# Twelve weight blocks converted inside attention in place of ten, two under way at a time, each loaded three units ahead

## The chip, the cores and the metric

One core of one Trainium2 chip. The time is device microseconds (us) of one execution. PE is the matrix engine (TensorE), "PEld" its weight loads, DVE is VectorE, ACT is ScalarE, POOL is GpSimd; SP issues nearly all DMAs. The outputs are float32. The weights of the two dense parts are stored as 64-bit floats.

## The reference, cut to what matters

```python
# attention: 4 batches, 8 heads, 576 queries and keys, head size 64
scores = scale * (q @ k.T)
scores = where(scores >= max(scores) - tau, scores, -1e9)
attn = exp(scores - max(scores)); attn = attn / (sum(attn) + 1e-9)
x = (attn @ v)            # gathered to 2304 tokens x 512
# first dense part, d_ff = 2048 (w_in, w_out)
h = x @ w_in
y = (h * tanh(softplus(h))) @ w_out
# second dense part, d_ff = 1536 (w_a, w_b, w_out)
out = ((y @ w_a) * (y @ w_b)) @ w_out
```

## The kernel before, in words

**Attention** is written as one loop over 80 units; its order on every engine is kept as written. A unit is 128 queries of two heads. The two heads of one batch make a round of five units, c0 to c4 (c4 holds the last 64 queries of both heads and is half as large), so there are 16 rounds. In step n of the loop:

- DVE copies the scores of unit n out of PSUM with a running minimum (`least`, L266, one per head), and applies the threshold to unit n-1 (`mask`, L285, one per head). In c2 it also scales an older pair's result (`send`, L362, tile `u`), and in the last four rounds, again in c2, it splits a piece of the next phase's input (`first_x`, L72 `xlfirst`).
- ACT takes the exponentials (L278) and copies transposed tiles out of PSUM (L322).
- PE transposes unit n-2 (L321, `tp`), multiplies unit n-4 with v (L340, L344, tile `sums_o`), and computes the scores of unit n+1 (L258, in c4 L260, tile `sp`). There are two `sp` buffers, one per head, so scores of unit n+1 wait until `least` has emptied those of unit n.

**Weights.** Each of the 68 weight blocks (128 x 512) is loaded as 64-bit words (L90, tile `raww`, two buffers) and turned by seven operations into a high and a low fp32r part: ACT L95 (`uw`), DVE L97 and L102 (`aw`), POOL L106 (adds `uw` into `aw`), ACT L108 (`fw`), DVE L110, ACT L112 (high part), DVE L114 (low part). The tiles `uw`, `aw`, `fw` have one buffer each. Blocks of w_in and w_out are called f_0 and f_1, for f = 0 to 15.

`convert` in the attention loop does the first blocks: it starts a block (only the load) at unit T0 = 1 and every PACE units after, and in each later step takes the number of operations that GROUPS lists. The rest are ordinary program after attention (`load_w1` in the first steps of the first dense part, then `after`). Outside attention the framework's scheduler orders the instructions by its own estimate of the time, and it also lets work of the dense part into the last units of attention.

**First dense part.** Tokens go in six tiles of 384. For each of 8 weight blocks f of a half, 12 matmuls make `hm` (L135 to L137, named hm_tile_f), ACT and DVE make `ghm` and `glm` (L178 to L180), and three steps later 12 matmuls add into four `acc` tiles, named with the tile and f of their input. The `acc` tiles take over PSUM that `sums_o` held. At the end of a tile ACT copies them out (L542). Before the last pair's `send` DVE waits for a DMA (`inv`).

Of the kernel before, what the change touches and what calls it, by code (L numbers as in the profile page):

```python
# [22 lines left out]
DFF1, DFF2 = 2048, 1536  # L23
FC1, FC2 = DFF1 // 128, DFF2 // 128
WA, WB = 16, 20
T0, PACE, EARLY = 1, 8, 5
NM = 384
TILES = NT // NM
SCALE = 1.0 / 8.0
# [5 lines left out]
def tile_attn_mish_bilinear(ctx, tc, qd, kd, vd, vd2, tau, w_in, w_out, w_a, w_b, w_out2, out):  # L35
    nc = tc.nc
    V, A, G, PE = nc.vector, nc.scalar, nc.gpsimd, nc.tensor
# [36 lines left out]
    def weight(pool, bufs, src, name, lo_eng):  # L74

        shape = [128, CC, 128]
        out = pool.tile([128, 2, CC, 128], F32R, tag="w", name=name, bufs=bufs)
        tl = lambda s, dt: cv.tile(shape, dt, tag="cv" + s, name=s + name, bufs=1)
        if src.dtype == F32:
            f = tl("f", F32)
            nc.sync.dma_start(out=f, in_=src)
        else:
            raw = cv.tile([128, CC, 256], U32, tag="wraw", name="raw" + name, bufs=2)
            nc.sync.dma_start(out=raw, in_=src.bitcast(U32))  # L90
            words = raw.rearrange("p c (n t) -> p t c n", t=2)
            hi, lo = words[:, 1], words[:, 0]
            u, a, f = tl("u", I32), tl("a", I32), tl("f", F32)
            yield A
            A.activation(u, lo, AF.Copy, scale=2.0 ** -29)  # L95
            yield V
            V.tensor_scalar(  # L97
                out=a, in0=hi.bitcast(I32), scalar1=3, scalar2=0x3FFFFFF8,
                op0=ALU.logical_shift_left, op1=ALU.bitwise_and,
            )  # L100
            yield V
            V.scalar_tensor_tensor(  # L102
                out=a, in0=hi.bitcast(I32), scalar=-0x40000000, in1=a, op0=ALU.bitwise_and, op1=ALU.bitwise_or
            )
            yield G
            G.tensor_tensor(out=a, in0=a, in1=u, op=ALU.add)  # L106
            yield A
            A.activation(f, hi.bitcast(F32), AF.Square)  # L108
            yield V
            V.scalar_tensor_tensor(out=f, in0=f, scalar=TINY, in1=a.bitcast(F32), op0=ALU.is_ge, op1=ALU.mult)  # L110
        yield A
        A.activation(out[:, 0], f, AF.Copy)  # L112
        yield lo_eng
        lo_eng.tensor_tensor(out=out[:, 1], in0=f, in1=f32(out[:, 0]), op=ALU.subtract)  # L114
        return [(out[:, 0, c], out[:, 1, c]) for c in range(CC)]
# [7 lines left out]
    def w1_stages(f, i, pool, bufs, eng):  # L123
        w, block = ((w_in, column_block), (w_out, row_block))[i]
        w1[f][i] = yield from weight(pool, bufs, block(w, f), f"w1{f}_{i}", eng)
# [58 lines left out]
    with late_pools:  # L184
# [188 lines left out]
                split(*x0[c], xs["raw"], V)  # L373

        conv = [w1_stages(f, i, wa_p, WA, V) for f in range(EARLY) for i in range(2)]
        GROUPS = (0, 1, 1, 1, 2, 1, 1, 1)
        active = []

        def convert(start):

            for item in list(active):
                stages, k = item
                for _ in range(GROUPS[k]):
                    if next(stages, None) is None:
# [83 lines left out]
    def w2_steps():  # L468
        slots = iter([(wb_p, WB)] * 4 + [(wa_p, WA)] * 16 + [(wb_p, WB)] * 16)
        for f in range(FC2):  # L470
            for i, (w, block) in enumerate(((w_a, column_block), (w_b, column_block), (w_out2, row_block))):
                stages = weight(*next(slots), block(w, f), f"w2_{f}_{i}", V)
                while True:
                    try:
                        next(stages)
                    except StopIteration as end:
                        w2[f][i] = end.value
                        break
                yield
# [157 lines left out]
```

## Time and profile before

| | |
|---|---|
| time, median of 3 runs | 1163.65 us (1163.05 to 1164.02) |
| the profiled execution's own time | 1163.93 us |
| its span, first to last instruction | 1162.0 us |
| granted PE clock, mean | 0.996 |
| busy over the span: PE, PEld, DVE, ACT, POOL | 98%, 89%, 53%, 47%, 13% |
| attention, to the last scores of PE; first matmul of the dense part | 282.43 us; 286.76 us |

A busy PE is not PE at its peak: ends of matmuls are modelled, so spacing from start to start says more than busy time. The clock column gives the granted PE clock of a stretch as a part of 2.4 GHz (0.50 is 1.2 GHz). DVE and ACT are busy in the first 415 us and mostly idle after it.

### The profile page before, as it was taken

What the parts mean: (1) busy time and instruction counts of PE and PEld (TensorE: products, weight loads), DVE (VectorE), ACT (ScalarE), POOL (GpSimd) and SP (SyncE); (2) the same over time, 40 slices, a digit from 0 to 9 for tenths busy, and PEclk for the clock granted to TensorE, in tenths of its full rate; (3) what the DMA queues carried; (4) which work ended last, traced back from release to release, by engine and by line L of the source; (5) the groups of instructions that cost most, each with busy time, mean ns of one, the idle gap of its engine ahead of it and who ended that gap; (6) DMA issues with size and microseconds to landing.
All of it is one profiled execution on the core that took longest, in us unless ns stands there. A gap on an engine that the chain in (4) does not pass through costs nothing.

```text
span 1162.0 us, 18631 instructions
## 1 busy us (share of the span) xinstructions
PE 1140.0 (98%) x7154; PEld 1038.2 (89%) x7154; DVE 616.9 (53%) x1236; ACT 548.5 (47%) x1111; POOL 148.0 (13%) x154
## 2 busy tenths in 40 slices
PE   9999999999899999999999999999999999999998
PEld 7666666666799999999999999999999999999998
DVE  6899898888699951797222187412121121121111
ACT  6888888877676753575222255312121121221211
POOL 1222222211133320232000023100000000000000
PEclk9999999999999999999999999999999999999999
DMA  4535545534455531465112154101010010100000
GB/s 146 147 108 160 150 123 154 165 115 146 125 169 157 166 124 42 131 203 160 61 49 68 56 177 149 46 1 55 1 56 1 1 56 1 46 9 1 28 1 28
DMA packets 65943, 104.03 MB, mean 90 GB/s; under 512 B 5696, under 2 KB 49984, under 8 KB 65856
## 3 DMA queue, kind: packets, MB, share of 16 engines
q1 hardware_dynamic: 65568, 102.56, 28.6%
q8 instruction: 56, 0.92, 0.3%
q10 hardware_dynamic: 288, 0.30, 0.1%
q14 instruction: 31, 0.25, 0.1%
HBM read 83.89 MB, written 18.95 MB: 88 GB/s over the span
## 4 chain that ended last, share of the span: by engine, by line
PE 74%; DVE 10%; ACT 6%; DMA 5%; issue 4%; POOL 1%; SPq 0%; DVEq 0%; ACTq 0%; POOLq 0%
PE acc L135 8%; PE acc L136 8%; PE acc L137 7%; PE sums_o L340 5%; PE sp L258 5%; PE tp L321 5%; PE hb L135 4%; PE ha L137 4%; PE ha L135 4%; PE hb L137 4%; PE ha L136 4%; PE hb L136 4%; PE hm L135 3%; PE hm L137 3%; PE hm L136 3%
## 5 line engine op out<-in xcount | busy, mean ns | idle before, releaser
L569 DVE TENSOR_TENSOR s<-hb,s 128x384 f32<-128x384 f32 x72 | 40.1, 557 | 275.5 <-PE hb L137 275.5
L106 POOL TENSOR_TENSOR aw<-aw,uw 128x512 int32<-128x512 int32 x68 | 105.9, 1557 | 364.1 <-DVE aw L102 321.6
L180 DVE TENSOR_TENSOR glm<-hsm,ghm 128x384 fp32r<-128x384 f32 x96 | 81.5, 849 | 107.9 <-ACT ghm L179 107.7
L135 PE MATMUL acc<-ghm,w 128*128 128x384 f32 x384 | 130.4, 340 | 5.3 <-ACT y L542 3.1
L136 PE MATMUL acc<-glm,w 128*128 128x384 f32 x384 | 129.4, 337 | 0.0
L137 PE MATMUL acc<-ghm,w 128*128 128x384 f32 x384 | 129.3, 337 | 0.0
L568 ACT ACTIVATE s<-ha 128x384 f32<-128x384 f32 x72 | 35.3, 490 | 186.9 <-PE ha L137 186.9
L266 DVE TENSOR_SCALAR_CACHE_REDUCE s<-sp 128x576 f32<-128x576 f32 x144 | 103.8, 754 | 28.4 <-PE sp L258 24.3
L137 PE MATMUL hm<-xhm,w 128*128 128x384 f32 x352 | 118.0, 335 | 0.0
L135 PE MATMUL hm<-xhm,w 128*128 128x384 f32 x352 | 118.0, 335 | 0.0
L136 PE MATMUL hm<-xlm,w 128*128 128x384 f32 x352 | 118.0, 335 | 0.0
L278 ACT ACTIVATE ex<-s,m 128x576 f32<-128x576 f32 x144 | 109.3, 771 | 9.9 <-DVE s L266 9.5
L322 ACT ACTIVATE pt<-tp 128x512 f32<-128x512 f32 (+1 forms) x192 | 91.3, 488 | 26.4 <-PE tp L321 24.7
L285 DVE SCALAR_TENSOR_TENSOR pm<-s,te,ex 128x576 f32<-128x576 f32 x128 | 99.4, 814 | 0.0
L135 PE MATMUL acc<-gh,w 128*128 128x384 f32 x288 | 96.3, 336 | 2.3 <-DVE y L540 1.6
L71 ACT ACTIVATE gh<-s 128x384 fp32r<-128x384 f32 x72 | 37.7, 523 | 127.5 <-DVE s L569 127.5
L178 ACT ACTIVATE hsm<-hm 128x384 f32<-128x384 f32 x96 | 46.6, 486 | 107.5 <-PE hm L137 107.5
L136 PE MATMUL acc<-gl,w 128*128 128x384 f32 x288 | 96.7, 336 | 0.5 <-DVE gl L72 0.5
L135 PE MATMUL ha<-xhy,w 128*128 128x384 f32 x288 | 96.6, 335 | 0.0
L137 PE MATMUL ha<-xhy,w 128*128 128x384 f32 x288 | 96.6, 335 | 0.0
L136 PE MATMUL ha<-xly,w 128*128 128x384 f32 x288 | 96.6, 335 | 0.0
L137 PE MATMUL hb<-xhy,w 128*128 128x384 f32 x288 | 96.6, 335 | 0.0
(86 smaller groups left out, 2421.6 us busy)
## 6 DMA issues: line engine op xcount, KB each, us to landing
raww<-w_out SPq DMA_DIRECT2D x28, 512.0 KB
v<-vd SPq DMA_DIRECT2D x16, 576.0 KB
raww<-w_in SPq DMA_DIRECT2D x16, 512.0 KB
raww<-w_a SPq DMA_DIRECT2D x12, 512.0 KB
raww<-w_b SPq DMA_DIRECT2D x12, 512.0 KB
xrm<-xd SPq DMA_DIRECT2D x28, 192.0 KB
v<-vd SPq DMA_DIRECT2D x16, 320.0 KB
qr<-qd SPq DMA_DIRECT2D x15, 320.0 KB
```

What stands on the lines that cost most here:

```text
L106: G.tensor_tensor(out=a, in0=a, in1=u, op=ALU.add)
L135: PE.matmul(ps, wh, xh, start=start, stop=False)
L136: PE.matmul(ps, wh, xl, start=False, stop=False)
L137: PE.matmul(ps, wl, xh, start=False, stop=stop)
L180: V.tensor_tensor(out=g[1], in0=hs, in1=f32(g[0]), op=ALU.subtract)
L258: PE.matmul(sp[:, half, 0:288], d["qs"][r, cols], d["k"][r, keys], start=True, stop=True)
L266: V.tensor_scalar(out=u["s"][:, h].rearrange("p (a c) -> p a c", a=2), in0=u["sp"][h][:, :, 0:288], scalar1=1.0, scalar2=None, op0=ALU.mul ...
L278: A.activation(u["e"][:, h], u["s"][:, h], AF.Exp, bias=u["m"][:, h:h + 1], scale=-1.0)
L285: V.scalar_tensor_tensor(out=u["pm"].rearrange("p a c -> p (a c)")[:, h * S:(h + 1) * S], in0=u["s"][:, h], scalar=u["te"][:, h:h + 1], in ...
L321: PE.transpose(tp[:, i], pm[:, j0 + i], ident)
L322: return lambda: A.activation(pt[:, j0:j0 + m], tp[:, :m], AF.Copy)
L340: PE.matmul(po[r], v[0][:, j + 4 * h, r], pair[pi][c & ~1][:, :, j + 4 * h], start=j == 0, stop=j == 4)
```

## The change

```diff
-T0, PACE, EARLY = 1, 8, 5
+T0, PACE, EARLY = 1, 6, 6
...
             nc.sync.dma_start(out=raw, in_=src.bitcast(U32))
             words = raw.rearrange("p c (n t) -> p t c n", t=2)
             hi, lo = words[:, 1], words[:, 0]
+            yield A
             u, a, f = tl("u", I32), tl("a", I32), tl("f", F32)
-            yield A
             A.activation(u, lo, AF.Copy, scale=2.0 ** -29)
...
-        GROUPS = (0, 1, 1, 1, 2, 1, 1, 1)
+        GROUPS = (0, 0, 1, 2, 2, 1, 1, 1)
```

A block now starts every 6 units in place of 8, and the blocks 0_0 to 5_1 (EARLY = 6) are done in the loop, in place of 0_0 to 4_1. Counted from its start unit, a block's L95 comes 3 units later (before: 2), L97 with L102 at 4 (before: 3 and 4), L106 with L108 at 5, L110 at 6, L112 at 7, L114 at 8, as before. The single tiles `uw`, `aw`, `fw` are taken at L95 and no longer at the load, so that the next block's load can be out before the last one is done. The block started at unit 67 is the last and ends at unit 75; before, the one started at 73 ended at 81.

How the instructions move, at three places. The first is DVE around c2 of the fifteenth round, from `least` of unit 72 to that of unit 74. Before (w_0_3102 is block 4_0):

```order
L266 TENSOR_SCALAR s_2_3379,m_2_3355<-sp_2_0_3359 128x576
L266 TENSOR_SCALAR s_2_3379,m_2_3355<-sp_2_1_3360 128x576
L285 SCALAR_TENSOR_TENSOR pm_1_3317,sm_3273<-s_1_3337,te_1_3316,ex_1_3347 128x576 x2
L362 TENSOR_TENSOR u_3037<-u_3037,inv_3194 128x576
L72 TENSOR_TENSOR xlfirst_169<-xr_3334,xhfirst_168 128x384
L266 TENSOR_SCALAR s_3_3424,m_3_3401<-sp_3_0_3404 128x576
L266 TENSOR_SCALAR s_3_3424,m_3_3401<-sp_3_1_3405 128x576
L114 TENSOR_TENSOR w_0_3102<-fw_0_3107,w_0_3102 128x512
L285 SCALAR_TENSOR_TENSOR pm_2_3358,sm_3273<-s_2_3379,te_2_3356,ex_2_3394 128x576 x2
```

With the change (aw_1_3365 is block 5_1, aw_0_3855 block 6_0, which is already the scheduler's):

```order
L266 TENSOR_SCALAR s_2_3418,m_2_3393<-sp_2_0_3397 128x576
L266 TENSOR_SCALAR s_2_3418,m_2_3393<-sp_2_1_3398 128x576
L285 SCALAR_TENSOR_TENSOR pm_1_3353,sm_3309<-s_1_3375,te_1_3352,ex_1_3385 128x576 x2
L362 TENSOR_TENSOR u_3070<-u_3070,inv_3230 128x576
L72 TENSOR_TENSOR xlfirst_169<-xr_3372,xhfirst_168 128x384
L266 TENSOR_SCALAR s_3_3464,m_3_3440<-sp_3_0_3443 128x576
L266 TENSOR_SCALAR s_3_3464,m_3_3440<-sp_3_1_3444 128x576
L110 SCALAR_TENSOR_TENSOR fw_1_3366<-fw_1_3366,aw_1_3365 128x512
L285 SCALAR_TENSOR_TENSOR pm_2_3396,sm_3309<-s_2_3418,te_2_3394,ex_2_3433 128x576 x2
L97 TENSOR_SCALAR aw_0_3855<-raww_0_3852 128x512
```

In unit 73 L110 of a block stands where L114 stood; its POOL addition (L106) is therefore in unit 72, beside `u`. A first operation of block 6_0 follows in the same unit.

The second place is DVE in units 76 and 77, c1 and c2 of the last round. Before (block 4_1 alone):

```order
L266 TENSOR_SCALAR s_1_3559,m_1_3538<-sp_1_0_3541 128x576
L266 TENSOR_SCALAR s_1_3559,m_1_3538<-sp_1_1_3542 128x576
L97 TENSOR_SCALAR aw_1_3467<-raww_1_3464 128x512
L285 SCALAR_TENSOR_TENSOR pm_0_3504,sm_3502<-s_0_3516,te_0_3501,ex_0_3531 128x576 x2
L266 TENSOR_SCALAR s_2_3601,m_2_3577<-sp_2_0_3581 128x576
L266 TENSOR_SCALAR s_2_3601,m_2_3577<-sp_2_1_3582 128x576
L102 SCALAR_TENSOR_TENSOR aw_1_3467<-raww_1_3464,aw_1_3467 128x512
L285 SCALAR_TENSOR_TENSOR pm_1_3540,sm_3502<-s_1_3559,te_1_3539,ex_1_3569 128x576 x2
L362 TENSOR_TENSOR u_3264<-u_3264,inv_3417 128x576
L72 TENSOR_TENSOR xlfirst_171<-xr_3556,xhfirst_170 128x384
```

With the change (w_0_3851 is block 6_0, aw_1_3869 block 6_1):

```order
L266 TENSOR_SCALAR s_1_3594,m_1_3573<-sp_1_0_3576 128x576
L110 SCALAR_TENSOR_TENSOR fw_0_3856<-fw_0_3856,aw_0_3855 128x512
L266 TENSOR_SCALAR s_1_3594,m_1_3573<-sp_1_1_3577 128x576
L285 SCALAR_TENSOR_TENSOR pm_0_3538,sm_3536<-s_0_3551,te_0_3535,ex_0_3566 128x576 x2
L97 TENSOR_SCALAR aw_1_3869<-raww_1_3866 128x512
L114 TENSOR_TENSOR w_0_3851<-fw_0_3856,w_0_3851 128x512
L102 SCALAR_TENSOR_TENSOR aw_1_3869<-raww_1_3866,aw_1_3869 128x512
L266 TENSOR_SCALAR s_2_3635,m_2_3612<-sp_2_0_3616 128x576
L266 TENSOR_SCALAR s_2_3635,m_2_3612<-sp_2_1_3617 128x576
L285 SCALAR_TENSOR_TENSOR pm_1_3575,sm_3536<-s_1_3594,te_1_3574,ex_1_3604 128x576 x2
L362 TENSOR_TENSOR u_3300<-u_3300,inv_3457 128x576
L110 SCALAR_TENSOR_TENSOR fw_1_3870<-fw_1_3870,aw_1_3869 128x512
```

Four operations of the scheduler's blocks 6_0 and 6_1 stand in unit 76 where one stood, and one in unit 77 as before. Up to the `least` of unit 79 DVE now has all four operations of fourteen blocks and one of a fifteenth, in place of nine blocks and two operations of the tenth.

The third place is PE at the end of hm_0_5, the sixth product of the first tile. Before:

```order
L135 MATMUL hm_0_5_4041<-xhfirst_170,w_0_3823 128x384
L136 MATMUL hm_0_5_4041<-xlfirst_171,w_0_3823 128x384
L137 MATMUL hm_0_5_4041<-xhfirst_170,w_0_3823 128x384
L135 MATMUL acc_0_3964<-ghm_0_0_3818,w_1_614 128x384
L136 MATMUL acc_0_3964<-glm_0_0_3819,w_1_614 128x384
L137 MATMUL acc_0_3964<-ghm_0_0_3818,w_1_614 128x384
```

With the change:

```order
L137 MATMUL hm_0_5_4041<-xhfirst_170,w_0_2949 128x384
L135 MATMUL hm_0_6_4072<-xhfirst_164,w_0_3851 128x384
...
L137 MATMUL hm_0_6_4072<-xhfirst_170,w_0_3851 128x384
L135 MATMUL hm_0_7_4131<-xhfirst_164,w_0_3898 128x384
L136 MATMUL hm_0_7_4131<-xlfirst_165,w_0_3898 128x384
L137 MATMUL hm_0_7_4131<-xhfirst_164,w_0_3898 128x384
L135 MATMUL hm_0_7_4131<-xhfirst_166,w_0_3898 128x384
L135 MATMUL acc_0_3964<-ghm_0_0_3846,w_1_525 128x384
```

All 12 matmuls of hm_0_6 and 4 of hm_0_7 come ahead of the first `acc`; before, hm_0_6 came 36 matmuls of `acc` later.

## Rows read from the trace of the kernel before

**Rows 1.** Busy time by stretch; columns: PE, PEld, DVE, ACT, POOL (instructions), clock, DMA

```profile
0.00:282.43 282.43, 274.54 (x2170) 181.75 (x2170) 247.23 (x653) 229.26 (x464) 57.00 (x93) 0.99 0.47 141
...
412.00:1162.00 750.00, 741.74 (x4265) 739.49 (x4265) 257.26 (x420) 230.47 (x472) 48.20 (x33) 1.00 0.18 59
```

**Rows 2.** Timeline of PE, scores of units c0 alone; columns: start, length

```profile
21.79 1.24 PE L258 MATMUL sp<-k,qs 64*128 64x288 f32 x8
...
38.63 1.24 PE L258 MATMUL sp<-k,qs 64*128 64x288 f32 x8
...
73.13 1.24 PE L258 MATMUL sp<-k,qs 64*128 64x288 f32 x8
...
91.62 1.24 PE L258 MATMUL sp<-k,qs 64*128 64x288 f32 x8
...
108.46 1.24 PE L258 MATMUL sp<-k,qs 64*128 64x288 f32 x8
...
126.16 1.24 PE L258 MATMUL sp<-k,qs 64*128 64x288 f32 x8
...
177.25 1.24 PE L258 MATMUL sp<-k,qs 64*128 64x288 f32 x8
...
194.66 1.24 PE L258 MATMUL sp<-k,qs 64*128 64x288 f32 x8
...
211.74 1.24 PE L258 MATMUL sp<-k,qs 64*128 64x288 f32 x8
...
232.08 1.24 PE L258 MATMUL sp<-k,qs 64*128 64x288 f32 x8
...
250.34 1.24 PE L258 MATMUL sp<-k,qs 64*128 64x288 f32 x8
...
269.05 1.24 PE L258 MATMUL sp<-k,qs 64*128 64x288 f32 x8
```

**Rows 3.** Groups of DVE instructions until 282.43 us: busy us, mean ns

```profile
L266 DVE TENSOR_SCALAR_CACHE_REDUCE s<-sp 128x576 f32<-128x576 f32 x143 | 103.0, 754 | 28.3 <-PE sp L258 24.3
L285 DVE SCALAR_TENSOR_TENSOR pm<-s,te,ex 128x576 f32<-128x576 f32 x124 | 96.3, 814 | 0.0
...
L102 DVE SCALAR_TENSOR_TENSOR aw<-raww,aw 128x512 int32<-128x512 int32 x10 | 6.9, 688 | 0.0
```

**Rows 4.** Line L362: duration ns, minimum, median, maximum

```profile
L362 DVE TENSOR_TENSOR u<-u,inv x16: 751/754/1826, 49.7 to 314.8; 128x576 f32<-128x576 f32 x16
```

**Rows 5.** Timeline of DVE and POOL, unit 22 (c2 of the fifth round)

```profile
84.21 1.83 DVE L362 TENSOR_TENSOR u<-u,inv 128x576 f32<-128x576 f32 x1
...
83.55 1.87 POOL L106 TENSOR_TENSOR aw<-aw,uw 128x512 int32<-128x512 int32 x1
```

**Rows 6.** Timeline of PE in attention; in brackets: idle before, and releaser

```profile
88.88 1.37 PE L321 MATMUL tp<-ident,pm 128*128 128x128 f32 x8 [0.76 <-ACT u L349]
...
225.85 1.24 PE L260 MATMUL sp<-k,qs 128*128 128x288 f32 x4 [0.80 <-DVE s L266]
...
227.96 1.82 PE L321 MATMUL tp<-ident,pm 128*128 128x128 f32 x8 [0.77 <-ACT u L349]
```

**Rows 7.** Stretches of 25 us around the two falls of the clock

```profile
225.00:250.00 25.00, 22.47 (x163) 14.40 (x163) 20.91 (x56) 19.42 (x40) 3.69 (x7) 0.93 0.59 174
300.00:325.00 25.00, 21.78 (x129) 20.43 (x126) 16.29 (x27) 12.78 (x28) 6.45 (x5) 0.93 0.48 148
```

**Rows 8.** Timeline of PE at the start of the first dense part

```profile
295.55 0.65 PE L321 MATMUL tp<-ident,ph 128*128 128x128 f32 x4 [0.80 <-ACT pt L322]
...
309.50 0.44 PE L135 MATMUL acc<-ghm,w 128*128 128x384 f32 x1 [2.26 <-ACT u L349]
...
323.94 0.44 PE L135 MATMUL hm<-xhfirst,w 128*128 128x384 f32 x1 [0.96 <-ACT w L112]
```

**Rows 9.** Waits from 320 to 430 us: total us, times, longest

```profile
PE acc L135 <- ACT y L542: 2.0, 3, 0.7
```

**Rows 10.** Timeline of DVE, the last pair's send

```profile
314.81 0.76 DVE L362 TENSOR_TENSOR u<-u,inv 128x576 f32<-128x576 f32 x1 [5.24 <-DMA inv<-rd]
```

## The prediction

> **What bounds the kernel now.** I read the stretches first. After 412 us PE does 4265 matmuls in 750 us, one in 0.176 us, with next to no gap [rows 1]; nothing of the change reaches there. Attention is less plain: until 282 us PE counts as busy for 274.5 us, DVE for 247.2 and ACT for 229.3 of 282.4 [rows 1]. So I took the rhythm of PE, the starts of the scores of c0. Two of the rounds shown take 16.84 us (from 21.79 and from 91.62) and none less [rows 2]; a floor that comes back to the hundredth I take for PE's own work. From 21.79 to 269.05 us lie 14 rounds, 247.26 us, where 14 floors make 235.76: attention loses 11.5 us, and it loses them in single rounds. Which conversion work fell into a round tells what each kind costs, and that is my price list.
>
> **Price list** (round time less 16.84) [rows 2].
> - POOL's addition L106 falls in c2, beside `u`: units 20 to 24 take 18.49, a loss of **1.65**. There `u` took 1.83 us, where 0.75 is usual, and ended with the addition (83.55 to 85.42) [rows 4, 5]. This happened twice in 16 (`u` at most 1826 ns); the other case, with a split in the same unit, is units 60 to 64: 20.34, a loss of **3.50**, of which about 1.75 is PE at half clock (25 us at a mean of 0.93) [rows 7].
> - A split in c2 without that: 1.42 (65 to 69) and 1.87 (70 to 74, with L114 in c3).
> - L114 in c3: 17.70, 0.86 (30 to 34). L97 in c2 and L102 in c3: 17.41, 0.57 (50 to 54). One such operation in c2: 17.08, 0.24 (55 to 59).
>
> The reason is visible in the loads of DVE. In c2 it has two copies of 0.75, two masks of 0.81 and `u`, 0.75 [rows 3, 4]; neighbours overlap by some 0.08, so 3.5 us, when a unit lasts 3.37 on average. What is added there is late in c3 and holds back the next scores and transposes.
>
> **The change, part by part.**
>
> *Loads three units ahead.* They can only save waits of ACT for `raww`; their worth is within the rounds below. SP issues as many DMAs as before, in another order.
>
> *Positions.* Block j starts at 1+6j, so its L106 is in unit 6+6j (before 6+8j). In c2 that is j = 1, 6, 11: units 12, 42, 72. Before it was j = 2, 7: units 22, 62. Three collisions in place of two, and the third again meets a split (units 62, 67, 72, 77 have one). L97 and L102 now follow each other, 1.2 us at 0.69 each as an upper bound [rows 3]; they meet c2 or c3 in four rounds.
>
> *Rounds from unit 5 to 74, new.* Two collisions, 1.65 each, and 0.3 each because L97 precedes L102 just ahead of them: 3.9. Collision with split, 3.5 and 0.3: 3.8. Four rounds with L97 and L102 in c2 or c3 (15, 20, 45, 50), 0.57 each: 2.3. L114 in c2 (25, 55) and L110 in c2 (35), 0.24 each: 0.7. L114 in c3 (30): 0.86. Units 60 to 64, split with L114 in c3: 1.87. Units 65 to 69, split with L110: 1.42. Units 5 to 9: none. Sum 14.85, against 11.50: **+3.3 us**.
>
> *The last round.* Blocks 6_0 and 6_1 now come here. In unit 76 DVE has two copies, two masks and four conversion operations: 1.35 + 1.48 + 4 x 0.55 = 5.0 us. In unit 77 it has 3.5, one operation of 0.6 and the split, 0.5: 4.6. With 3.4 us a unit, DVE is 2.8 late at unit 78. Of the 1.07 + 0.61 late in units 20 to 24, PE paid 1.65, so lateness at c3 is paid nearly whole; with 0.4 for what DVE has in hand in unit 75, 2.4. Bounds: nothing, since the last round held two such operations and a split before too, and its last scores came 13.4 us after 269.05, four units at 3.35; and 2.8. I take **+2.4**, as units 20 to 24 are the nearest rows.
>
> *The start of the dense part.* PE waits 2.26 us for the first `acc`, until ACT's L349 has emptied `sums_o`, and then runs at half clock: 25 us at 0.93 are 1.75 lost [rows 7, 8]. With the change 16 matmuls, 16 x 0.176 = 2.8 us, stand ahead of that `acc`, and block 6_0 that they need is done in unit 76. The wait is covered if L349 is no later. On ACT it now follows the last small copy by eight instructions in place of ten. Gain 2.26 + 1.75 = **4.0** (bounds 0 and 4.0). The wait of 0.96 for hm_0_7's weights [rows 8] goes, as 7_0 is now among the blocks begun in attention: **1.0** (bounds 0 and 1.0). The wait of 0.80 at 295.55 for a copy of ACT [rows 8] should go, since fewer conversions stand before that copy: **0.8** (bounds 0 and 0.8).
>
> *Later.* DVE and ACT have four to five blocks less between 315 and 412 us. The three waits of 0.7 for ACT's L542 are at ends of tiles [rows 9]; the last of them falls after conversion has ended: **0.7**.
>
> **Sum** against the profiled 1163.93: + 3.3 + 2.4 - 4.0 - 1.0 - 0.8 - 0.7 = -0.8, so 1163.1; the median lies 0.28 below the profiled execution. I forecast **1163.0 us, no change**.
>
> One page speaks against this reading. The Trainium skill, Perfetto Trace Analysis, section Identifying the Most-Contended Engine, says that matmul busy time is a poor measure and that busy time of weight loads tells how much room PE has. By it attention would leave PE a third of its time (181.75 of 282.43) [rows 1], and DVE would be the bound. By the spacing of the rounds the trace does not agree, since two rounds with different conversion work on DVE keep the same 16.84 us. By the page the time would be that of the last rival below.
>
> **Rivals.**
> - *PE falls to half clock more often* (slower). It fell after two waits of 0.80 and 0.77 in one round, and did not in the round with one of 0.76 [rows 6, 7]. The new collisions at units 12 and 42 and the late tail have waits of that order; each fall costs 1.75. It decides from two falls more than now: 1163.0 + 3.5 = 1166.5, with three 1168.2. For it: nothing fills PE there. Against: the same collision at unit 22 left the clock whole.
> - *The tail is paid nowhere* (faster). DVE's lateness in units 76 to 78 may be absorbed by the matmuls of hm that already stand between the last transposes, and the collision at unit 72 may come without a fall: -2.4 and -1.75 give 1160.6 and 1158.9. Against: the scores of units 78 and 79 stand ahead of any hm.
> - *The gap moves.* PE comes to `acc` of f = 5 some 5 us earlier, but their low parts stand on DVE behind the last `u`, which waits 5.24 us for the DMA `inv` until 314.8 [rows 10]. I count 2 to 3 us in hand; if `inv` is that much later, 1 to 3 us return: 1164 to 1166.
> - *DVE is the bound in attention.* Then about 4.7 blocks more, at four operations of 0.6, cost 11 us where I count 5.7: 1168.3. Against: the equal rounds.
>
> **How the numbers follow.** Chances: forecast 0.44, tail unpaid 0.27, half clock 0.14, gap moves 0.10, DVE bound 0.05. No change means within 0.2%, about what can be told from nothing here: 1161.3 to 1166.0. The forecast's own range is 1161.3 to 1165. Faster 0.27. The moved gap lies mostly inside: same 0.50. The rest is slower: 0.23. The range for 8 in 10 takes in the tail unpaid and two falls of the clock: 1159.0 to 1167.5.
>
> **What the profile would show.** `u` of about 1.8 us at three places, units 12, 42 and 72, and rounds there longer by 1.7, 1.7 and 3.5. Scores of unit 79 about 5.7 us later than 282.43. No wait of PE for L349, none for hm_0_7, and no half clock near 310 us. Conversions ending some 12 us before 412. I am wrong if the last scores come before 285 us, if the clock falls more than once in attention, or if PE waits for a `glm` after 315 us.

## The result, and where the time went

The changed kernel takes **1176.88 us** (median of 4 runs, 1175.77 to 1177.17) against 1163.66 us for the kernel before on the same chip: a ratio of 1.0112, 95% interval 1.0097 to 1.0127. It is 13 us slower, where I forecast no change. The profiled execution spans 1175.0 us, 13.0 more than before.

To see where, I laid the matmuls of the dense part side by side in order (the first of the new kernel against the first of the old, and so on) and read by how much the new ones lag:

| place | lag, us | it changed because of |
|---|---|---|
| scores of unit 75 | +3.3 | the attention rounds |
| scores of unit 79 | +7.65 | the last round |
| 48th matmul of the dense part | +8.75 | a wait for ACT's copy of a transpose, 1.89 us where it was 0.80 |
| 144th to 240th (329 to 345 us) | +3.9 | the hole at L349 and the wait for hm_0_7 are gone |
| 264th, after the end of the first tile | +11.3 | a wait for ACT's L542, and half clock |
| 456th, after the end of the second tile | +13.9 | the same again, smaller |
| 648th, after the end of the third tile | +12.8 | a wait of before [rows 9] is gone |
| last | +13.0 | |

At 345 us the lag is 3.9 us, where the terms of the prediction up to there add up to -0.1. The larger part of the loss, 9.1 us, is made behind that, at the ends of the first two tiles, where the prediction had only a gain of 0.7.

The scores that answer to [rows 2], in the timeline of PE (start, length): unit 75 and unit 79.

```profile
272.32 1.24 PE L258 MATMUL sp<-k,qs 64*128 64x288 f32 x8
...
290.08 1.24 PE L260 MATMUL sp<-k,qs 128*128 128x288 f32 x4
```

PE's waits in the dense part that answer to [rows 8, 9], in the same view:

```profile
300.81 0.66 PE L321 MATMUL tp<-ident,pm 128*128 128x128 f32 x4 [1.89 <-ACT pt L322]
...
352.77 0.69 PE L135 MATMUL acc<-ghm,w 128*128 128x384 f32 x1 [5.97 <-ACT y L542]
...
390.45 0.44 PE L135 MATMUL acc<-ghm,w 128*128 128x384 f32 x1 [2.05 <-ACT y L542]
```

The waits of 2.26 and 0.96 us of [rows 8] have gone. In their place stand 5.97 and 2.05 us at L542, where [rows 9] had at most 0.7. The clock follows (stretches; the column behind POOL is the granted clock). In attention it never falls. At each of the two waits it goes to 1.2 GHz for a while: for 6.8 us from 350.9, when the first wait still had 1.9 us to run, and for 3.4 us from 391.8, behind the second.

```profile
340.00:365.00 25.00, 19.03 (x97) 18.71 (x96) 18.84 (x33) 17.53 (x36) 9.35 (x6) 0.86 0.61 187
385.00:410.00 25.00, 22.95 (x123) 22.55 (x122) 20.63 (x27) 14.78 (x32) 7.38 (x5) 0.93 0.46 143
...
0.00:290.08 290.08, 275.56 (x2170) 180.65 (x2170) 258.14 (x670) 237.35 (x479) 64.62 (x98) 1.00 0.49 146
```

Why are the copies L542 late? The kernel before shows how close it was: there PE waited 0.66 us for them (timelines of ACT, PE).

```profile
343.08 0.85 ACT L542 ACTIVATE y<-acc 128x384 f32<-128x384 f32 x2
```

```profile
343.61 0.44 PE L135 MATMUL acc<-ghm,w 128*128 128x384 f32 x1 [0.66 <-ACT y L542]
```

ACT takes its instructions in order, and the scheduler has put conversions ahead of the copies: 23 L112 stand before the first L542 (19 before the change). What ACT waits for in that stretch is the next view, waits of ACT from 320 to 430 us, first of the kernel before (total, times, longest):

```profile
ACT fw L108 <- DVE w L114: 9.1, 16, 1.2
```

and of the changed one:

```profile
ACT fw L108 <- DVE w L114: 33.3, 17, 5.9
```

L108 needs the only `fw` tile, which DVE's L114 of the block before gives back. And L114 stands on DVE behind the last pair's `u`, which waits for `inv` as in [rows 10], 8.8 us later. The chain in the timelines of DVE and then ACT:

```profile
323.62 0.76 DVE L362 TENSOR_TENSOR u<-u,inv 128x576 f32<-128x576 f32 x1 [6.02 <-DMA inv<-rd]
324.29 0.68 DVE L114 TENSOR_TENSOR w<-fw,w 128x512 fp32r<-128x512 f32 x1
```

```profile
325.01 0.66 ACT L108 ACTIVATE fw<-raww 128x512 f32<-128x512 f32 x1 [5.92 <-DVE w L114]
...
346.37 0.67 ACT L108 ACTIVATE fw<-raww 128x512 f32<-128x512 f32 x1 [1.50 <-DVE w L114]
...
351.68 0.66 ACT L95 ACTIVATE uw<-raww 128x512 int32<-128x512 uint32 x1
352.23 0.87 ACT L542 ACTIVATE y<-acc 128x384 f32<-128x384 f32 x2
```

Between `u` and the copies lie seven conversions, 28.6 us (323.62 to 352.23). Before, it was also seven and 28.3 us, from 314.81 [rows 10] to 343.08. So PE came to the end of the tile 3.9 us late, the copies 9.1 us late. Two other differences cancel further on: the clock falls once more at 736.6 us, for 3.4 us, and two waits of PE that the kernel before has near 735 us are gone.

### The profile page after: what moved, and what is told of

It is laid out like the page before. It is cut to its first block, busy times and chain, and to the rows that moved or that the text cites. A ratio compares the mean times of both kernels' runs of the same rounds, so it can differ in the third digit from the quotient of the medians.

```text
span 1175.0 us, 18627 instructions
## 1 busy us (share of the span) xinstructions
PE 1142.8 (97%) x7154; PEld 1041.0 (89%) x7154; DVE 610.5 (52%) x1236; ACT 544.5 (46%) x1111; POOL 147.6 (13%) x154
## 3 DMA queue, kind: packets, MB, share of 16 engines
q1 hardware_dynamic: 65568, 102.56, 28.3%
HBM read 83.89 MB, written 18.95 MB: 88 GB/s over the span
## 4 chain that ended last, share of the span: by engine, by line
PE 79%; DVE 8%; ACT 5%; DMA 4%; issue 3%; POOL 1%; SPq 0%; ACTq 0%; DVEq 0%; POOLq 0%
PE acc L135 9%; PE acc L137 8%; PE acc L136 8%; PE sums_o L340 5%; PE sp L258 5%; PE tp L321 5%; PE hm L137 4%; PE hb L135 4%; PE hb L136 4%; PE hb L137 4%; PE hm L135 4%; PE hm L136 4%; PE ha L136 4%; PE ha L137 4%; PE ha L135 4%
## 5 line engine op out<-in xcount | busy, mean ns | idle before, releaser
L106 POOL TENSOR_TENSOR aw<-aw,uw 128x512 int32<-128x512 int32 x68 | 105.3, 1549 | 379.0 <-DVE aw L102 351.6
L180 DVE TENSOR_TENSOR glm<-hsm,ghm 128x384 fp32r<-128x384 f32 x96 | 67.0, 699 | 119.0 <-ACT ghm L179 118.8
L135 PE MATMUL acc<-gh,w 128*128 128x384 f32 x288 | 96.9, 338 | 2.0 <-DVE y L540 2.0
L321 PEld LDWEIGHTS tp<-ident,pm 128*128 128x128 f32 x576 | 63.3, 141 | 39.5 <-ACT ex L278 9.2
L137 PE MATMUL acc<-gh,w 128*128 128x384 f32 x288 | 96.8, 337 | 0.0
L71 ACT ACTIVATE gh<-s 128x384 fp32r<-128x384 f32 x72 | 37.7, 524 | 127.1 <-DVE s L569 127.1
```

The lines of the kernel that those rows point to most:

```text
L135: PE.matmul(ps, wh, xh, start=start, stop=False)
L137: PE.matmul(ps, wl, xh, start=False, stop=stop)
L180: V.tensor_tensor(out=g[1], in0=hs, in1=f32(g[0]), op=ALU.subtract)
L321: PE.transpose(tp[:, i], pm[:, j0 + i], ident)
```

## The experiments

All diffs are against the changed kernel unless another is named. The ratio behind a time, with its 95% interval, is against the kernel before on the same chip; its medians there were 1162.8 to 1163.2 us. "Hoisted" are blocks 6_0 and 6_1, which the scheduler moved from the ordinary program into the last round.

**1. Nothing hoisted into the last round.** The same blocks, six units later.

```diff
-T0, PACE, EARLY = 1, 6, 6
+T0, PACE, EARLY = 7, 6, 6
```

> The same twelve blocks every six units, begun six units later, so that each stands where its neighbour stood (collisions still in units 12, 42 and 72) and the last one ends in unit 81: blocks 6_0 and 6_1 can no longer run in the last round. Both theories: scores of unit 75 at about 272.3, last scores 285.7 to 287 (before 282.4, changed kernel 290.1). Queue theory (the copies of the first tile's result, L542, come a fixed 28.6 us after the load of the last inv has landed, since on ACT they stand behind seven conversions that wait for DVE, which waits for inv): inv at about 318, copies at 346 to 347, PE still waits 5 to 8 us there, total 1170 to 1173. Tail theory (the hoisted blocks are the whole loss): no wait of PE over 2 us for L542, total 1161 to 1164.

Measured: 1167.23 us, 1.0036 (1.0023 to 1.0049). Scores of unit 75 at 273.13, of unit 79 at 286.89: the last round lost 4.0 us less. PE still waits at the end of the tile (timelines of DVE, PE):

```profile
317.76 0.76 DVE L362 TENSOR_TENSOR u<-u,inv 128x576 f32<-128x576 f32 x1 [4.41 <-DMA inv<-rd]
...
345.72 0.69 PE L135 MATMUL acc<-ghm,w 128*128 128x384 f32 x1 [4.59 <-ACT y L542]
```

The tail theory falls. The copies start at 345.18, 27.4 us behind `u`. The total is below the queue theory's range (1170 to 1173): the wait at the end of the second tile went too.

**2 and 3. The last `u` out of DVE's way**, in the changed kernel and in the one before. `issue_after` places an instruction behind the named one in its engine's order.

```diff
-        V.tensor_tensor(out=g[1], in0=hs, in1=f32(g[0]), op=ALU.subtract)
+        low[0] = V.tensor_tensor(out=g[1], in0=hs, in1=f32(g[0]), op=ALU.subtract)
...
-            if half == 0 and t == 0 and f == 4:
-                send_last()
+            if half == 0 and t == 1 and f == 4:
+                with tc.issue_after(low[0].ins): send_last()
```

> The changed kernel with the last pair's multiplication u (L362) queued on DVE behind the low part glm of tile 1, f = 4, so that DVE no longer waits for inv in the first tile. Nothing changes before 310 us: last scores at 290. Queue theory: the 6.0 us of DVE go, conversions run on, the copies L542 come at 345 to 347, PE's wait of 5.97 us falls under 1 us and the half clock behind it goes; the next wait (2.05) may shrink too: total 1165 to 1170. Rival (conversions are paced by their own loads and by the loop between ACT, DVE and POOL, not by inv): copies within 1 us of 352, total 1175.5 to 1177.

Measured: 1167.51 us, 1.0043 (1.0029 to 1.0057), so 9 us of the 13 gone. ACT's order is unchanged, and the copies come 6.2 us earlier; the first wait falls to 0.4 us, both stretches of half clock at these waits are gone, and the second wait stays (timelines of ACT, PE):

```profile
346.06 0.87 ACT L542 ACTIVATE y<-acc 128x384 f32<-128x384 f32 x2
...
381.95 0.44 PE L135 MATMUL acc<-ghm,w 128*128 128x384 f32 x1 [2.05 <-ACT y L542]
```

> The kernel before with the same late u. Queue theory: DVE's wait of 5.24 us goes, the copies of tile 0 come at 338 to 340 in place of 343.1, PE's waits for L542 (2.0, 3 and 0.7 in the rows) shrink: total 1159 to 1162. Rival (own pace of the conversions): no change, 1162.5 to 1165.

Measured: 1162.54 us, 0.9991 (0.9981 to 1.0001). A miss for the queue theory: the time is in the rival's range, at its lower end. The copies come 1.9 us earlier (341.17), but in this profile PE comes nearly as much earlier, and its three waits are 0.5, 1.5 and 0.6: nothing clear is gained. In that kernel the copies and PE arrive together, and `inv` costs nothing that the run can show.

**4. The loads alone.** Ten blocks every eight units, with the new `yield` and GROUPS.

```diff
-T0, PACE, EARLY = 1, 6, 6
+T0, PACE, EARLY = 1, 8, 5
```

> Ten blocks every eight units as before, with only the other part of the change: loads three units ahead, the tiles uw, aw, fw taken at L95, L95 one unit later and L97 together with L102. If the change's loss comes from blocks per round alone: attention within 1.5 us of before (282.4), total 1162 to 1165.5. If the early loads or the single tiles themselves make ACT wait (as L95 of block 6_1 waited 2.64 us for its load): waits of ACT for raww in attention and a total over 1166.

Measured: 1163.75 us, 1.0005 (0.9995 to 1.0014). In the total the early loads neither cost nor give.

**5. Shifted blocks and the late `u`** (1 and 2 together).

> The shifted twelve blocks (nothing hoisted into the last round) together with the late u. Queue theory: the wait of 4.59 us for L542 and the 3.4 us of half clock behind it, which the shifted kernel still had at 341 us, go: 1167.2 - 4.6 - 3.4 = 1159.2, range 1158 to 1162, and this is the first form of the change that is not slower than before. If another wait takes their place (the loop of the conversions, loads): 1164 to 1167.

Measured: 1166.0 us, 1.0027 (1.0016 to 1.0037); a miss. DVE no longer waits, but a load now holds ACT, and the copies come at 344.66, only 0.5 earlier (timelines of ACT, PE):

```profile
319.31 0.67 ACT L95 ACTIVATE uw<-raww 128x512 int32<-128x512 uint32 x1 [3.49 <-DMA raww<-w_in]
...
345.21 0.69 PE L135 MATMUL acc<-ghm,w 128*128 128x384 f32 x1 [3.78 <-ACT y L542]
```

So the theory was too narrow: `inv` is one of the things that can hold the conversions. What remains in every kernel is that the copies stand behind them.

**6. The copies ahead of later conversions.** Blocks 9_0 to 15_1 are placed on ACT behind the copies of the tile before; `inv`, loads and attention stay as they are.

```diff
-                    A.activation(y, acc[c], AF.Copy)
+                    kept[0] = A.activation(y, acc[c], AF.Copy)
...
-                    load_w1(FC1 // 2 + (t * FC1 // 2 + f) // TILES, wb_p, WB, V)
+                    with tc.issue_after(kept[0].ins) if t else ExitStack(): load_w1(FC1 // 2 + (t * FC1 // 2 + f) // TILES, wb_p, WB, V)
```

> The changed kernel, its twelve blocks and their places in attention untouched, but the conversions of blocks 9_0 to 15_1 are queued on ACT behind the copies L542 of the tile before, so that 18 conversions stand ahead of the first copies in place of 23, whatever inv does. Nothing changes before 320 us (last scores at 290). If the loss behind 340 us is that the copies stand in ACT's order behind too many conversions: copies at 347, as soon as PE is there, no wait of PE over 0.7 us for L542, no half clock between 340 and 400 us; 1176.9 - 5.97 - 3.4 - 2.05 - 1.7 = 1163.8, range 1161 to 1167. If PE waits there for something else than ACT's order (the conversions are pushed to where they collide): 1170 or more.

Measured: 1166.35 us, 1.0028 (1.0018 to 1.0038), inside the range and 2.5 above the sum. All four copies run at once, as soon as the last `acc` before them is done, and PE waits for nothing from 320 to 430 us (timeline of ACT; then PE's stretches, full at full clock):

```profile
341.25 1.81 ACT L542 ACTIVATE y<-acc 128x384 f32<-128x384 f32 x4
```

```profile
340.00:365.00 25.00, 25.00 (x146) 25.00 (x145) 9.88 (x18) 12.50 (x26) 2.57 (x2) 1.00 0.27 90
385.00:410.00 25.00, 25.00 (x147) 25.00 (x146) 10.82 (x20) 12.24 (x26) 2.89 (x2) 1.00 0.27 86
```

Most of what is above the sum is, by the trace, a price of the edit. The conversions that it holds back push later ones on: the 52nd L112 comes at 582.4 us in place of 544.6. At the end of a tile at 580 us, where the changed kernel has no wait, DVE's addition L540 now stands behind conversions, and these behind a load (timelines of ACT, DVE, PE):

```profile
577.84 0.67 ACT L95 ACTIVATE uw<-raww 128x512 int32<-128x512 uint32 x1 [3.12 <-DMA raww<-w_b]
```

```profile
579.06 0.69 DVE L114 TENSOR_TENSOR w<-fw,w 128x512 fp32r<-128x512 f32 x1
579.67 0.55 DVE L540 TENSOR_TENSOR y<-acc,y 128x384 f32<-128x384 f32 x1
```

```profile
580.28 0.44 PE L135 MATMUL acc<-ghm,w 128*128 128x384 f32 x1 [2.27 <-DVE y L540]
```

Half clock for 3.4 us follows it. All five kernels with this edit have the wait (1.7 to 2.3 us at 571 to 580 us), and none of the others. In its place a wait of 1.0 to 1.1 us for L542, at 511 to 526 us in the others, is gone.

The same edit of the kernel before:

> The kernel before with the same queueing (18 conversions ahead of the first copies in place of 19). Its three waits of 0.7 for L542 should go, 2 us, and no more: 1160.5 to 1162.5. If conversions that are now later make PE wait for weights: 1164 or more.

Measured: 1160.5 us, 0.9981 (0.9971 to 0.9990), as expected. And of the shifted kernel of experiment 1:

> The shifted twelve blocks (nothing hoisted into the last round) with the same queueing. The late u left a wait of 3.78 us there because a load and the loop of the conversions held the copies in place of inv; with the copies ahead that wait of 4.59 and its 3.4 of half clock go whatever holds the conversions: 1167.2 - 4.6 - 3.4 = 1159.2, range 1157.5 to 1161.5. If the wait stays over 2 us, the order on ACT is not the cause.

Measured: 1160.22 us, 0.9977 (0.9968 to 0.9986), 7.0 us below experiment 1. The late `u` had given 1.2 there. In all three kernels the waits for L542 go with the order on ACT, whatever holds the conversions: that order is their cause.

**7. Where an operation falls in the round.** Each block meets a round alike, with nothing in c2 and c3.

```diff
-T0, PACE, EARLY = 1, 6, 6
+T0, PACE, EARLY = 15, 5, 6
...
-        GROUPS = (0, 0, 1, 2, 2, 1, 1, 1)
+        GROUPS = (0, 0, 0, 2, 1, 2, 0, 0, 1, 1, 1)
```

> Twelve blocks, one every five units, from unit 15 on, so that every block meets the round alike: L95 and L97 in c4, L102 in c0, L106 and L108 in c1, L110 in c4, L112 in c0, L114 in c1; nothing in c2 and c3, and no addition of POOL beside u. If where an operation falls in the round sets what it costs: rounds of 16.84 to 17.1 without a split, 1.2 to 1.5 more with one, scores of unit 75 at 260 to 263 (before 269.05), and u 0.75 everywhere. The u stays early, so the queue theory has the copies L542 27 to 29 us behind inv, and PE still waits 4 to 6 us there: total 1155 to 1159. Rival (DVE is the bound in attention, as many operations cost as much wherever they stand): unit 75 at 272 or later, total 1166 or more.

Measured: 1164.24 us, 1.0017 (1.0008 to 1.0027). Rounds without a block take 16.84 us, rounds with one 17.83, with a split 18.3 (timeline of PE, scores of units 10 and 15, then of 25 and 30):

```profile
39.18 1.24 PE L258 MATMUL sp<-k,qs 64*128 64x288 f32 x8
...
56.02 1.24 PE L258 MATMUL sp<-k,qs 64*128 64x288 f32 x8
...
89.70 1.24 PE L258 MATMUL sp<-k,qs 64*128 64x288 f32 x8
...
107.53 1.24 PE L258 MATMUL sp<-k,qs 64*128 64x288 f32 x8
```

The total is above the expected range, and attention gained about a quarter of what I expected: unit 75 comes at 269.39, against 272.32. In this layout a block costs 0.99 us a round, so c4, c0 and c1 are not free. They are not the best places either: in the changed kernel all eight operations of block 0_0 (those listed for a weight block in the section on the kernel before, which calls them seven) run between the scores of units 5 and 10, from L95 at 21.83 to L114 at 37.54 us, with L110 in c2 and L112 in c3, and that round takes 16.87 us (timeline of PE):

```profile
21.68 1.24 PE L258 MATMUL sp<-k,qs 64*128 64x288 f32 x8
...
38.55 1.24 PE L258 MATMUL sp<-k,qs 64*128 64x288 f32 x8
```

Units 35 to 39, which a later block meets in the same way, take 17.13. No run has every block there. The copies stand 28.1 us behind `u`, with a wait of 5.15 us. With the late `u`:

> The same positions and the late u. Queue theory: the wait for L542 and its half clock go as well, 7 to 8 us less than the kernel with the positions alone: 1148 to 1152. Rival (something else holds the end of the first tile): 1154 or more.

Measured: 1161.96 us, 0.9991 (0.9981 to 1.0000), a miss, in the rival's range; the wait is still 2.93. With fourteen blocks and the late `u`:

> As the kernel before it in this call, with fourteen blocks from unit 5 on, every five units (the last ends in unit 81 too). If the rounds take two more blocks at no cost: unit 75 within 1 us of the kernel with twelve, conversions end some 8 us earlier, and the time is the same to 2 us less. If DVE has come to its limit in attention: unit 75 later by 2 us or more.

Measured: 1164.1 us, 1.0013 (1.0004 to 1.0023). From unit 5 to 75 it takes 249.0 us in place of 247.0 (nine rounds at 17.82 to 17.84 in place of seven): 0.99 us a block again. With twelve blocks, the early `u` and the copies first:

> The places in the round (nothing in c2 and c3) with the same queueing and the early u. The wait of 5.15 us, its 1.7 of half clock and the 0.7 at 412 us go: 1164.2 - 5.15 - 1.7 - 0.7 = 1156.7, range 1155 to 1159.

Measured: **1156.83 us, 0.9949 (0.9935 to 0.9964)**: faster than both kernels. That it meets the sum is partly luck: the three waits named went, a wait of 2.17 us at 571 us and two stretches of half clock (3.4 us each) came, and later waits of 1.0, 1.7 and 0.5 us, which I had not counted, went as well.

**8. What the last round paid for.** Blocks 6_1, 7_0 and 7_1 are held until the last exponential on ACT and the last mask on DVE (`ends`); 6_0 stays.

```diff
+    LATE = ((6, 1), (7, 0), (7, 1))
...
+            with tc.issue_after(ends[0].ins) if (f, i) in LATE else ExitStack(), tc.issue_after(ends[1].ins) if (f, i) in LATE else ExitStack():
```

> The changed kernel with block 6_1, and the two blocks behind it, held on ACT and DVE until the last exponential and the last mask; block 6_0 stays hoisted into the last round. Units 75 to 79 took 17.8 us in the changed kernel and 13.8 where nothing was hoisted. Load theory (the 4.0 us are a chain: L95 of block 6_1 waits 2.64 us on ACT for its load, ACT's copies, exponentials and L108 of block 6_0 behind it, L110 on DVE behind that, and least behind L110): 13.5 to 15. Rival, as the prediction had it (DVE is late by the number of its operations): block 6_1 brought three of the seven conversion operations, so 15.7 to 16.3. PE's end of the first tile is the same as in the changed kernel either way.

Measured, scores of units 75 and 79 (timeline of PE; one run):

```profile
274.05 1.24 PE L258 MATMUL sp<-k,qs 64*128 64x288 f32 x8
...
287.47 1.24 PE L260 MATMUL sp<-k,qs 128*128 128x288 f32 x4
```

13.42 us, as before the change (13.38), just under the load theory's range: block 6_0 costs nothing there, all 4.4 came with 6_1 and what followed it. In the changed kernel the trace reads so (timelines of ACT, DVE and PE): L95 of 6_1 waits on ACT for its load, L108 of 6_0 is behind it, and behind that two paths lead to PE. On ACT itself L350 follows, for which PE waits 1.97 us before L340, with the scores of unit 77 right behind. On DVE the second `least` of unit 76 stands behind L110; it ended at 281.75, when PE was still at L340. So PE's wait that ended last was the one for ACT.

```profile
276.77 0.67 ACT L95 ACTIVATE uw<-raww 128x512 int32<-128x512 uint32 x1 [2.64 <-DMA raww<-w_out]
...
279.64 0.64 ACT L108 ACTIVATE fw<-raww 128x512 f32<-128x512 f32 x1
```

```profile
280.39 0.69 DVE L110 SCALAR_TENSOR_TENSOR fw<-fw,aw 128x512 f32<-128x512 f32 x1 [2.71 <-ACT fw L108]
281.00 0.75 DVE L266 TENSOR_SCALAR_CACHE_REDUCE s<-sp 128x576 f32<-128x576 f32 x1
```

```profile
280.60 1.52 PE L340 MATMUL sums_o<-pt,v 128*64 128x256 f32 x12 [1.97 <-ACT u L350]
282.05 1.24 PE L258 MATMUL sp<-k,qs 64*128 64x288 f32 x8
```

The scores of units 76 and 77 are 6.4 us apart (275.64 and 282.05) where 3.35 is usual, so up to here 3.1 of the 4.4 us are lost. The next unit loses 1.3 more, where L108 of 6_1 waits for the `fw` tile and PE for a small copy behind it (timelines of ACT, PE):

```profile
284.20 0.68 ACT L108 ACTIVATE fw<-raww 128x512 f32<-128x512 f32 x1 [1.16 <-DVE w L114]
```

```profile
285.10 0.66 PE L321 MATMUL tp<-ident,pm 128*128 128x128 f32 x4 [1.03 <-ACT pth L319]
```

The run holds block 6_1 back whole; the load's part against that of 6_1's own operations is read from the trace and not isolated by a run.

The time was 1175.2 (one run; 1164.14 before): with PE earlier and the copies at 348.06, PE waits 7.33 there.

**9. POOL's addition out of c2**, for the three blocks that met `u` there (`item[2]` is the number of the block, 1, 6 and 11 here).

```diff
-        GROUPS = (0, 0, 1, 2, 2, 1, 1, 1)
+        GROUPS = ((0, 0, 1, 2, 2, 1, 1, 1), (0, 0, 1, 2, 0, 2, 2, 1))
...
-                for _ in range(GROUPS[k]):
+                for _ in range(GROUPS[item[2] % 5 == 1][k]):
```

> The changed kernel, with POOL's addition L106 of the blocks begun in units 7, 37 and 67 moved from c2 into c3 with L108, L110 and L112 into c4 and L114 into c0. If the addition beside u is what those rounds pay (as predicted, 1.65 us each): u 0.75 us everywhere, rounds 10 to 14 and 40 to 44 at 17.2 to 17.9 in place of 18.95, rounds 70 to 74 at 18 to 18.4 in place of 19.42. If it is the bare number of operations in c2 and c3: 18.7 or more.

Measured: `u` at most 757 ns in sixteen; units 10 to 14 take 17.28 (38.35 to 55.63) in place of 18.96, units 40 to 44 17.28 in place of 18.95, units 70 to 74 17.75 in place of 19.42: 1.67 us each. The edit also takes L110 out of c3, so this is the price of two things: of the collision, by which `u` alone grew 1.08, and of the L110 right behind it, about 0.6, as the prediction had split it (1.07 and 0.61); no run separates the two.

```profile
L362 DVE TENSOR_TENSOR u<-u,inv x16: 695/752/757, 49.9 to 316.9; 128x576 f32<-128x576 f32 x16
```

The time was 1170.11 (one run; 1164.14 before).

**10. All three causes out**: shifted, copies first, no collision.

> The shifted twelve blocks (nothing hoisted into the last round), the copies L542 ahead of the later conversions, and POOL's addition moved out of c2. The first two alone gave 1160.2. If the collisions are paid to the end once nothing behind them takes the time back, 3 x 1.67 = 5.0 us come off: 1155.2, range 1154 to 1157. If a later wait absorbs them: 1158 or more.

Measured: 1157.46 us, 0.9954 (0.9937 to 0.9970). 2.8 us under the first two alone, where 5.0 were expected. From unit 5 to 75 it is 4.9 faster, so the collisions do add up to there; but its unit 5 came 1.0 later (22.11 against 21.15, which differs from run to run). The profile of the kernel without this step had no half clock before its end, this one has two stretches of 3.4 us, behind waits of 2.1 us at 572 and 716 us (1.7 us each); the kernel without the step has the same two waits (2.0 and 2.1). That the clock accounts for the rest I read from two single profiles; no run isolates it.

## Why the prediction was wrong, step by step

- **Attention rounds, +3.3: right in the sum and in the price of a collision, by some luck in the parts.** Units 5 to 74 lose 14.88 us (272.32 - 21.68 - 235.76), where I summed 14.85. `u` took 1.83 us in units 12, 42 and 72, and such a round pays 1.67 (experiment 9; the step had 1.65). Other terms erred against each other: the third collision brought no half clock (2.6 where 3.8 stood), and units 65 to 69 lost 0.8 where 1.42 stood; the rounds with L97 and L102 in c2 or c3 lost 0.7 and 1.05 where 0.57 stood, and the first two collisions 2.1 each where 1.95 stood. One reading of mine was off: in unit 22 `u` did not end with the addition [rows 5]. It began at 84.21 and took 1.83, so it ended at 86.04, 0.62 us after the addition.
- **The last round, +2.4: it measured +4.4, and its mechanism was another.** The step argued from the number of DVE operations. Experiment 8 shows that those of block 6_0 cost nothing. What costs came with block 6_1, and the trace shows the wait for its load there, behind which ACT stood, and behind ACT both DVE and PE.
- **The start of the dense part: -4.0 and -1.0 came, -0.8 did not.** The holes at L349 and hm_0_7 are gone. The wait for a copy grew from 0.80 to 1.89: in the changed order L71 of xhm_1_0 stands ahead of the last exponential and waits 5.25 us for its load.
- **"Later", -0.7: this is the step that failed.** It said that DVE and ACT have four to five blocks less to convert; of the three waits at L542 it had the last one go, and the first two it left at 0.7, a change of nothing, without a reason. The last one went. The first two grew to 5.97 and 2.05 us, and with their half clock they cost 7.4 and 2.7 us, so that the step came to +9.1 (lag +3.9 to +13.0). ACT did 20 L112 between 315 and 412 us where it had done 22, so it was two blocks less, and the conversions ended 5 us earlier (409.3 against 414.2), not 12. I read [rows 9] as the price of a copy, and not as a sign that the copies had nothing in hand: at the end of a tile ACT's queue and PE arrived within 0.7 us of each other. The change moved PE 3.9 us later and the copies 9.1. The rival "the gap moves" had the right trigger, `inv` later on DVE, but followed it to `glm` only. It did not ask what stands behind L114 on ACT. Experiments 2 and 6 show the mechanism; 5 shows that `inv` is not the only thing that can hold the queue.
- **The signs of error that I named** (scores before 285 us, half clock in attention, a wait for `glm`) all stayed away, although the forecast failed: none looked at L542.
- The rival that DVE bounds attention did not come: unit 75 is where the price list put it.

The Trainium skill, TensorE: Matmul & The Clock Gate, section "Architectural detail: the array is 16× 32×32, not 1× 128×128", says that ScalarE and VectorE are strict first-in, first-out. The trace agrees: PE had stopped at 346.8 us, so the copies had their input by then, and they ran at 352.23, behind the conversions ahead of them. The Trainium skill, SBUF — State Buffer, section "SBUF: two separate sides", says that of an operation of DVE with two inputs in SBUF and one of GpSimd that reads SBUF, the one that starts first holds a shared pair of ports for its whole instruction and the other is blocked. The traces agree: `u` took 0.75 us alone (experiment 9) and 1.83 us where POOL's 1.87 had begun 0.66 before [rows 5]; it ended 0.62 after the addition.

## What to carry to other kernels

When work is moved to an earlier place, follow every in-order engine from there to the next instruction that the bounding engine waits for, and ask what is queued ahead of it; a small wait at such a place says that there is no slack, not that the price is small. A scheduler that orders by its own estimate of the time puts work whose inputs come late (a load, a round trip through DRAM) ahead of work that is urgent; an edge that keeps the urgent copy ahead was worth 7.0 us in one form here and 2.7 in the kernel before. It is not free: what it holds back runs later, and here it met the end of another tile (a wait of 1.7 to 2.3 us). And price added work by where it falls: here a block in attention cost between next to nothing (units 5 to 9 of the changed kernel) and 0.99 us a round (experiment 7), and a round paid 1.67 more where POOL read beside DVE and L110 followed in c3.

## What the runs showed that I had not expected

- One conversion block cost the same 0.99 us in each of seven rounds (17.82 to 17.84 against 16.84), though DVE had nothing added in c2 and c3. PE's waits in those rounds are of 0.6 us, five for ACT's copies and two for DVE's masks (89.7 to 214.5 us).
- After a wait of 0.76 us at the end of the round of units 70 to 74 the clock fell in experiment 8 (20.73 us for the round); in experiment 5, after the same wait of 0.76, it stayed whole (19.43).
